# Sliding-window attention with a dense two-layer network behind it: all scores in 64x64 quarters, keys transposed from paired heads, and another order of work in the head

## The chip, the cores and the metric

The kernel runs on one core of one Trainium2 chip. The metric is device time in microseconds (us) of one execution. One matmul engine (TensorE, "PE" in the profile) has a queue of its own, as have VectorE (DVE), ScalarE (ACT), GpSimd (POOL) and SyncE (SP). Each runs its instructions in program order and waits on semaphores for the others. PE reads SBUF and writes the accumulators in PSUM, which has eight banks.

## The reference

q, k and v have 8 batches, 8 heads, 576 positions and 64 channels. Cut to what matters:

```
scores = scale * q @ k.T                       # per batch and head
scores = where(abs(pos_q - pos_k) <= 32, scores, -1e9)
attn   = softmax(scores)                       # over keys
x      = (attn @ v), heads side by side        # 4608 tokens x 512
h      = x @ w_in                              # 512 -> 2048
out    = (h * sigmoid(1.702 * h)) @ w_out      # 2048 -> 512, float32
```

## The kernel before

The 4608 tokens are 36 units of 128 queries, each shifted by 32, so that unit u needs 64 + 64 + 64 keys. A unit has two blocks of 64 queries; each block needs 128 keys. Heads go in pairs: an even head lies on partitions 0 to 63 of `kT` and `qT`, the odd one on 64 to 127.

- `scores(u)` (L200) makes, for four head pairs and two blocks, a tile of keys by queries. In block 0 it does this with two matmuls per head pair, each on 64 rows by 128 columns of the PE array (the profile's form `64*128`, one for each head of the pair). In block 1 it uses four matmuls on 64 by 64 quarters (`64*64`), since there the two halves of the keys lie the other way round. So a unit has 24 matmuls, and the two forms take turns eight times a unit. ScalarE then takes exp (L218), `band(u)` on VectorE multiplies with the mask (L233).
- `values(u)` (L249) multiplies with v; `ve` holds the tokens 128u to 128u+127 and `vo`, which `odd_v` copies out of two `ve` tiles (L136, L137), those shifted by 64. `norm(u)` divides by the sum (L260, L261), and `x_T(u)` transposes x, on PE (L276) or, with no bank named, by a DMA that SyncE issues (L272). Two units make a tile xT[t] of 256 tokens.
- `layer1(t, d)` (L288, L290) is eight matmuls of 256 columns and one gelu; eight such chunks make t. `layer2(u, quarter)` (L299) is four matmuls of 512 columns; behind the fourth quarter VectorE copies the result out of PSUM (L303) and SyncE issues its store.
- `keys_T` and `queries_T` transpose a 512-token group of k and q for one head pair by eight PE transposes of 64 columns each (L145) and copy them into the rings `kT` and `qT`. From group 3 on q goes another way: `queries_cast` (L170) puts the heads of a pair side by side on VectorE, and `queries_X` (L175) transposes the whole group in one DMA. Where a ring wraps, `queries_wrap` (L180) copies its first columns behind its end and for that waits for the group's DMA.

PSUM banks have kinds: "h" (2 banks), "o" (1), "tp" (1), "a" (4). A tile of a kind waits until the last reader of the tile that had its bank is done. The first layer uses "h", the second "o" and "h", scores and values "a".

The order on each engine is written out by hand. `head()` sets up, issues the first loads on GpSimd's DMA queue, does the attention of units 0 to 3 alone, then layer 1 of t = 0 and 1, half of layer 2 of units 0 to 3, then attention of 4 to 6, then the other half. From then on `window(w)`, w = 4 to 19, does the attention of units 2w and 2w+1 around layer 2 of units 2w-4 and 2w-3, and then layer 1 of t = w-1. `feed(w)` prepares the `vo` tiles of the next window.

Of the kernel before, what the change touches and what calls it, by code (L numbers as in the profile page):

```python
# [27 lines left out]
class _Kernel:  # L28
# [29 lines left out]
    def bank(self, kind, shape, dtype, name):  # L58
        bufs = {"h": 2, "o": 1, "a": 4, "tp": 1}[kind]
        return self.ps.tile(shape, dtype, name=name, tag=kind, bufs=bufs)  # L60
# [19 lines left out]
    def setup_mask(self):  # L80

        nc, m = self.nc, self.mask
        lo, hi = slice(0, 64), slice(64, 128)
        nc.vector.memset(m, 1.0)
        for blks, rows, sign in ((slice(0, 2), lo, 1), (slice(0, 2), hi, -1), (slice(2, 4), lo, -1), (slice(2, 4), hi, 1)):
            ap = m[rows, blks, :].rearrange("p b (j s) -> p b j s", j=JT)
            nc.gpsimd.affine_select(out=ap, in_=ap, compare_op=ALU.is_ge, fill=0.0, base=0,
                                    pattern=[[0, 2], [-sign, JT], [-sign * JT, SQ // JT]], channel_multiplier=sign)
        cut = m.rearrange("p b (j s) -> p b j s", j=JT)
        for b, rows, cols in ((0, hi, slice(0, 8)), (0, lo, slice(8, 16)), (2, lo, slice(0, 8)), (2, hi, slice(8, 16))):  # L90
            nc.vector.memset(cut[rows, b, :, cols], 0.0)
# [57 lines left out]
    def keys_T(self, i, hp, kind="tp", eng=None):  # L149
        nc = self.nc  # L150
        tp = self.heads_T("k", i, hp, kind)
        at = (512 * i) % RING

        def put(dst, n):
            self.cast(eng or nc.vector, dst.rearrange("r (p j) -> r p j", j=JT),
                      tp[:, :, :n // JT].rearrange("r j p -> r p j"))

        put(self.kT[:, hp, at:at + 512], 512)
        if at == 0:
            put(self.kT[:, hp, RING:] if i else self.k_first[:, hp, :], 64)  # L160

    def queries_T(self, i, hp, kind="tp", eng=None):
# [4 lines left out]
    def queries_cast(self, i, hp, eng):  # L167
        if ("s", i) not in self.stage:
            self.stage["s", i] = self.work.tile([128, 4, JT, 2, self.D], BF16, name="qc", tag="qc")
        eng.tensor_copy(self.stage["s", i][:, hp],  # L170
                        self.stage["q", i][:, 2 * hp:2 * hp + 2, :].rearrange("p h (j d) -> p j h d", j=JT))

    def queries_X(self, i):
        at = (128 * i) % RP
        self.nc.sync.dma_start_transpose(self.qT[:, :, at:at + 128],  # L175
                                         self.stage["s", i].rearrange("p h j t d -> p (h j t d)"))
# [23 lines left out]
    def scores(self, u):  # L200
# [39 lines left out]
    def values(self, u):  # L240
        nc, D = self.nc, self.D
        p = self.p.pop(u)
        acc = [self.bank("a", [128, 4, D + 1], F32, f"pv{i}") for i in range(2)]
# [71 lines left out]
    def head(self):  # L315

        nc, dve, act = self.nc, self.nc.vector, self.nc.scalar
# [11 lines left out]
        for c in range(4):  # L329
            self.load_w_in(c)  # L330
        for c in range(2):
            self.load_w_out(c)
        for c in "kq":
            self.load_heads(1, c)
        self.load_v(4, 1)
        for m in range(5, 8):
            self.load_v(m)
        for c in range(2, 4):
            self.load_w_out(c)
        for c in "kq":  # L340
            self.load_heads(2, c)
        kinds = ("h", "tp", "h", "o")
        for hp in range(4):
            self.keys_T(0, hp, kinds[(2 * hp) % 4], dve)
            self.queries_T(0, hp, kinds[(2 * hp + 1) % 4], act)
# [8 lines left out]
        self.odd_v(1, dve)  # L354
        self.edge_T("k", "h", dve)
        self.edge_T("q", "h", act)
        self.values(1)
        self.x_T(0, "tp")
        self.norm(1)
        self.band(2)  # L360
        self.scores(3)
        self.odd_v(2, dve)
        self.values(2)
        self.x_T(1, "o")
        self.norm(2)
        self.band(3)
        self.odd_v(3, dve)
        self.values(3)
        self.x_T(2, "tp")
        self.norm(3)  # L370
        self.layer1(0, 0)
        self.x_T(3, "o")
        self.layer1(0, 1)
        self.layer1(1, 0)
        self.layer1(1, 1)
        dve.tensor_copy(self.v_first, self.ve[0][0:64])
        self.queries_wrap(0)
        for c in range(1, 4):
            for t in range(2):
                for d in (2 * c, 2 * c + 1):  # L380
                    self.layer1(t, d)
        kinds = ("h", "h", "o", "tp")
        for c in range(2):
            for u in range(4):
                self.layer2(u, c, kinds[u])
# [5 lines left out]
        self.odd_v(4, dve)  # L391
        self.odd_v(5, dve)
        self.odd_v(6, dve)
# [7 lines left out]
        self.band(6)  # L401
        self.x_T(4, "a")
        self.values(6)
        self.norm(6)
        self.x_T(5, "a")
        for u in range(4):
            self.layer2(u, 2)
        self.x_T(6, "a")
        for u in range(4):
            self.layer2(u, 3)  # L410
        for m in (8, 9, 10):
            self.load_v(m)
        for c in "kq":
            self.load_heads(3, c)
        for d in range(4):
            self.layer1(2, d)
        for hp in range(4):
            self.keys_T(2, hp, ("o", "tp")[hp % 2], dve)
            self.queries_T(2, hp, "a", act)
        for d in range(4, 8):  # L420
            self.layer1(2, d)
        for m in (7, 8, 9):
            self.odd_v(m, dve)
        for m in (11, 12, 13):
            self.load_v(m)

    def window(self, w):
# [3 lines left out]
        l2 = [(lambda u=u, i=i: self.layer2(u, i, ("o", "h")[u % 2]))  # L431
              for u in (2 * w - 4, 2 * w - 3) for i in range(4)]
        l1 = [(lambda d=d: self.layer1(w - 1, d)) for d in range(8)] if w <= self.NW else []
        if w == 4:
            heads = [(3, hp) for hp in range(4)]
        else:
            i = (w + 3) // 2
            heads = [(i, hp) for hp in ((0, 1) if w % 2 else (2, 3))] if 512 * i < self.N else []
# [6 lines left out]
        if w % 2 == 0 and 512 * (w // 2 + 2) < self.N:  # L445
            for c in "kq":
                self.load_heads(w // 2 + 2, c)
        if w == 4:
            self.scores(7)
            run(l2, 1)  # L450
            self.band(7)
        if att:
            self.scores(a)
        if w == 4:
            self.values(7)
            self.norm(7)
            self.x_T(7, "tp")
        for m in (2 * w + 6, 2 * w + 7):
            if 13 < m < self.NU:
                self.load_v(m)  # L460
        if att:
            self.scores(b)
        run(l2, 2)
        if w > 4:
            run(kt)
        run(l2, 2)
        if att:
            self.band(a)
        if w > 4:
            run(kt)  # L470
# [11 lines left out]
        if heads and w % 2:  # L482
            for hp in range(4):
                self.queries_cast(heads[0][0], hp, dve)
        if w == 4:
            for hp in range(4):
                self.queries_cast(3, hp, dve)
            self.queries_X(3)
        run(l2)
        run(l2)  # L490
        run(l1, 4)
        if w == 4:
            run(kt, 4)
        if w % 2 and heads:
            self.queries_X(heads[0][0])
# [66 lines left out]
```

## Time and profile before

| | us |
|---|---|
| median of 3 runs | 381.6 (380.46 to 382.26) |
| the profiled execution | 382.74 |
| its span, first to last instruction | 381.0 |
| PE busy (matmuls) | 347.7 |
| VectorE busy | 146.0 |
| ScalarE busy | 173.3 |
| GpSimd busy | 67.1 |

The span is shorter than the execution's own time by 1.7 us, which lie ahead of its first and behind its last instruction. Busy times are unions of an engine's instructions. The end of a matmul is modelled, so successive matmuls overlap in the rows, and how fast PE really goes is read from start to start. The granted clock is given as a share of 2.4 GHz: 1.00 is that level and 0.50 is 1.2 GHz.

### The profile page before, as it was taken

Reading aid. Unit: us, or ns where it says so; the run is one execution under the profiler, and the core shown is the slowest. Engines: PE = TensorE matmul, PEld = TensorE weight load, DVE = VectorE, ACT = ScalarE, POOL = GpSimd, SP = SyncE. Lnnn points to the kernel's source line nnn. Section 1 sums busy time; section 2 is a strip of 40 time slices with the busy share of each in tenths; the row PEclk is TensorE's granted clock in tenths of the full one; section 3 lists DMA queues with packets and bytes.
Section 4 is the critical chain, followed back from the end, with each engine's and each line's share of the span. In section 5 each row is a group of like instructions: output and inputs, shape, how many; then the busy total and the mean of one; then the engine's idle time right before and its main releaser. Section 6 shows DMA issues by size and latency. Waiting matters only on the chain.

```text
span 381.0 us, 8343 instructions
## 1 busy us (share of the span) xinstructions
PE 347.7 (91%) x3592; PEld 228.6 (60%) x3592; DVE 146.0 (38%) x427; ACT 173.3 (45%) x261; POOL 67.1 (18%) x94
## 2 busy tenths in 40 slices
PE   2849998998768999999999999999999999999995
PEld 1538855574453757575757575748474857666572
DVE  1662037343532525353444434342525250606001
ACT  2523634184242364545454554545463637382250
POOL 8834624100400104020401031110100000000000
PEclk9999995998998999999999999999999999999998
DMA  8999997922990929692969195908090211402011
GB/s 98 177 207 186 198 183 56 136 93 17 104 161 14 116 51 126 102 119 48 127 102 128 40 134 98 146 21 97 24 145 23 61 45 41 58 27 62 28 52 55
DMA packets 94429, 35.27 MB, mean 93 GB/s; under 512 B 67257, under 2 KB 89785, under 8 KB 94393
## 3 DMA queue, kind: packets, MB, share of 16 engines
q0 software_dynamic: 61760, 18.49, 51.4%
q1 hardware_dynamic: 32632, 16.26, 22.5%
q8 instruction: 28, 0.46, 0.5%
q14 instruction: 9, 0.07, 0.0%
HBM read 36.96 MB, written 9.44 MB: 122 GB/s over the span
## 4 chain that ended last, share of the span: by engine, by line
PE 75%; DVE 14%; DMA 6%; issue 2%; ACT 1%; POOL 1%; DVEq 0%; POOLq 0%
PE h_ps L288 31%; PE o_ps L299 29%; PE sc L212 9%; DMA qT<-qc 4%; DVE p L233 3%; DVE x L261 3%; PE pv L249 3%; DVE o_sb L303 3%; PE tp L145 2%; DMA qs<-in_q_dram 2%; DVE qc L170 2%; DVE kT L95 2%; DVE rec L260 1%; PE tp L276 1%; ACT p L218 1%
## 5 line engine op out<-in xcount | busy, mean ns | idle before, releaser
L290 ACT ACTIVATE g<-h_ps 128x512 bf16<-128x512 f32 x144 | 86.0, 597 | 167.8 <-PE h_ps L288 167.8
L299 PE MATMUL o_ps<-w_out_sb,g 128*128 128x512 bf16 x576 | 138.5, 390 | 0.0
L288 PE MATMUL h_ps<-xT,w_in_sb 128*128 128x256 bf16 x1152 | 132.9, 275 | 4.7 <-DVE o_sb L303 4.7
L288 PEld LDWEIGHTS <-w_in_sb 128*128 128x128 bf16 x1152 | 113.6, 99 | 23.9 <-issue 5.8
L299 PEld LDWEIGHTS <-g 128*128 128x128 bf16 x576 | 53.5, 100 | 61.7 <-issue 5.9
L95 DVE COPY kT<-tp 128x512 bf16<-128x512 bf16 (+2 forms) x45 | 25.6, 594 | 120.7 <-PE tp L145 120.7
L129 POOL DMA_DIRECT2D ve<-in_v_dram x40 | 33.8, 853 | 198.8 <-DVE rec L260 125.1
L303 DVE COPY o_sb<-o_ps 128x512 f32<-128x512 f32 x36 | 24.8, 689 | 75.7 <-PE o_ps L299 74.6
L212 PE MATMUL sc<-qT,kT 64*64 64x64 bf16 (+1 forms) x864 | 44.9, 215 | 2.3 <-DVE qT L180 2.3
L218 ACT ACTIVATE p<-sc 128x512 bf16<-128x512 f32 x70 | 36.7, 600 | 11.2 <-PE sc L212 11.1
L212 PEld LDWEIGHTS <-kT 64*64 64x64 bf16 (+1 forms) x864 | 30.9, 102 | 18.1 <-issue 6.0
L261 DVE TENSOR_TENSOR x<-pv,rec 128x256 bf16<-128x256 f32 x72 | 30.5, 424 | 2.5
L233 DVE TENSOR_TENSOR p<-p,mask 128x512 bf16<-128x512 bf16 x70 | 26.5, 418 | 6.0 <-ACT p L218 5.5
L249 PEld LDWEIGHTS <-p 128*64 128x64 bf16 x576 | 14.3, 118 | 18.6 <-DVE p L233 9.1
L145 PE MATMUL tp<-ident,ks 128*64 128x128 bf16 x288 | 15.8, 234 | 10.1 <-DMA ks<-in_k_dram 7.1
L249 PE MATMUL pv<-ve,p 128*64 128x65 bf16 x288 | 19.2, 208 | 5.7 <-DVE p L233 3.8
L145 PEld LDWEIGHTS <-ks 128*64 128x64 bf16 x288 | 10.4, 115 | 20.9 <-issue 9.7
L249 PE MATMUL pv<-vo,p 128*64 128x65 bf16 x288 | 18.5, 207 | 3.2 <-DVE vo L137 2.7
L290 ACT ACT_TABLE_LOAD x16 | 20.5, 1283 | 0.3
L218 ACT ACT_TABLE_LOAD x15 | 19.2, 1283 | 0.3
L95 ACT COPY qT<-tp 128x512 bf16<-128x512 bf16 (+1 forms) x13 | 7.2, 570 | 16.6 <-PE tp L145 16.4
L260 DVE RECIPROCAL rec<-pv 128x4 f32<-128x4 f32 x72 | 12.5, 173 | 2.2 <-PE pv L249 1.9
(36 smaller groups left out, 93.0 us busy)
## 6 DMA issues: line engine op xcount, KB each, us to landing
out_dram<-o_sb SPq DMA_DIRECT2D x70, 128.0 KB
ve<-in_v_dram POOLq DMA_DIRECT2D x32, 128.0 KB, 5.3
w_in_sb<-in_moe_w_in_dram POOLq DMA_DIRECT2D x4, 512.0 KB, 9.8
w_out_sb<-in_moe_w_out_dram POOLq DMA_DIRECT2D x4, 512.0 KB, 12.1
ks<-in_k_dram POOLq DMA_DIRECT2D x4, 256.0 KB, 6.1
qs<-in_q_dram POOLq DMA_DIRECT2D x4, 256.0 KB, 7.4
ks<-in_k_dram POOLq DMA_DIRECT2D x2, 448.0 KB, 13.8
qs<-in_q_dram POOLq DMA_DIRECT2D x2, 448.0 KB, 14.8
```

The lines of the kernel that those rows point to most:

```text
L95: (eng.copy if eng is self.nc.scalar else eng.tensor_copy)(out, in_)
L129: self.nc.gpsimd.dma_start(self.ve[m % NV][off:off + n, :, :self.D], self.v[b, :, s:s + n, :].rearrange("h s d -> s h d"))
L145: self.nc.tensor.transpose(tp[64 * t:64 * t + 64, j, :], self.stage[c, i][:, 2 * hp + t, j * self.D:(j + 1) * self.D], self.ident)
L212: nc.tensor.matmul(sc[eo][lo:lo + m, 2 * hp + blk, :], self.kT[r, hp, at:at + m], self.qT[r, JT * hp:JT * hp + JT, q0:q0 + 16], start=(n = ...
L218: nc.scalar.activation(p[:, eo], sc[eo], AF.Exp, scale=self.scale)
L233: self.nc.vector.tensor_mul(pv, pv, msk.to_broadcast([128, 4, 2, SQ]))
L249: nc.tensor.matmul(acc[half][blk * 64:blk * 64 + 64, hh, :], p[:, h % 2, h // 2 * 2 + blk, :], vt[:, h, :D + 1], start=(hh == 0), stop=(hh ...
L261: nc.vector.tensor_mul(x[:, hs, :], acc[half][:, :, :D], rec[:, hs, :].to_broadcast([128, 4, D]))
L288: nc.tensor.matmul(hps[:, i, :], self.w_in_sb[:, kr, ff * 128:(ff + 1) * 128], self.xT[t][:, kr, :], start=(i == 0 and kr == 0), stop=(i = ...
L290: nc.scalar.activation(self.g[t][:, 2 * d:2 * d + 2, :], hps, AF.Gelu_apprx_sigmoid)
L299: nc.tensor.matmul(o_ps, self.g[t][:, ff, s * 128:(s + 1) * 128], self.w_out_sb[:, ff, :], start=(ff == 0), stop=(ff == self.NFF - 1))
L303: nc.vector.tensor_copy(o_sb, o_ps)
```

## The change

It has four parts.

1. `scores` uses four 64x64 quarters in both blocks: 32 matmuls a unit and one form.
2. Keys of groups 3 and later are first put side by side by head pair on VectorE (`pair_heads`, the former `queries_cast`), and then transposed by four full 128x128 transposes.
3. The head is put in another order: the four `odd_v` of units 0 to 3 and the mask's memsets go to GpSimd, between the loads; layer 1 begins after units 0 and 1, with units 2 and 3 between its first chunks; attention of units 4 to 6 stands between chunks of layer 2 ("output-layer atoms"); the attention of window 4 (units 7 to 9) likewise.
4. In the windows, pairing q and its DMA go from between norm and the last layer-2 chunks into `feed`, behind `odd_v`, with the pairing of k; the loads of k and q stand a group earlier.

```diff
 # scores(u)
-                parts = ((0, 64, k0 + 64), (64, 64, k0)) if blk else ((0, 128, k0),)
-                for lo, m, at in parts:
+                for half in range(2):
+                    lo, at = 64 * half, k0 + 64 * (half ^ blk)
                     for eo in range(2):
                         r = slice(eo * 64, eo * 64 + 64)
-                        nc.tensor.matmul(sc[eo][lo:lo + m, 2 * hp + blk, :], self.kT[r, hp, at:at + m],
+                        nc.tensor.matmul(sc[eo][lo:lo + 64, 2 * hp + blk, :], self.kT[r, hp, at:at + 64],
 # keys_T(i, hp)
+        if ("k", i, "c") in self.stage:
+            tp = self.bank(kind, [128, JT, 128], BF16, "tp")
+            for j in range(JT):
+                self.nc.tensor.transpose(tp[:, j, :], self.stage["k", i, "c"][:, hp, j], self.ident)
+        else:
+            tp = self.heads_T("k", i, hp, kind)
 # pair_heads(c, i, hp, eng), was queries_cast
+        eng.tensor_copy(self.stage[c, i, "c"][:, hp],
+                        self.stage[c, i][:, 2 * hp:2 * hp + 2, :].rearrange("p h (j d) -> p j h d", j=JT))
 # head(): loads
+        self.load_w_in(0)
+        self.load_w_in(1)
+        self.odd_v(0, pool)
+        self.odd_v(1, pool)
+        self.load_w_in(2)
+        self.odd_v(2, pool)
+        self.odd_v(3, pool)
+        self.load_w_in(3)
+        self.cut_mask()
...
 # head(): the start of the work
         self.scores(0)
         self.scores(1)
+        self.edge_T("k", "h", dve)
+        self.edge_T("q", "h", act)
         self.band(0)
-        self.odd_v(0, dve)
         self.band(1)
         self.scores(2)
-        self.values(0)
+        self.values(0, "hh")
         self.norm(0)
...
+        self.scores(3)
+        self.values(1, "ot")
         self.norm(1)
+        self.x_T(0, "h", act)
+        self.x_T(1, "h", act)
         self.band(2)
+        self.layer1(0, 0)
         self.values(2)
         self.norm(2)
         self.band(3)
+        self.layer1(0, 1)
         self.values(3)
         self.norm(3)
+        self.layer1(0, 2)
+        self.x_T(2, "t")
+        self.layer1(0, 3)
         self.x_T(3, "o")
...
 # head(): run(n) issues the next n chunks of layer 2 of units 0 to 3
+        run(4)
         for hp in range(4):
             self.keys_T(1, hp, "a", dve)
             self.queries_T(1, hp, "a", act)
+            run(1)
         self.scores(4)
         self.scores(5)
...
         self.band(4)
+        run(3)
         self.band(5)
+        run(2)
         self.values(4)
         self.norm(4)
         self.scores(6)
+        self.band(6)
+        run(1)
         self.values(5)
         self.norm(5)
+        run(1)
         self.x_T(4, "a")
+        run(1)
+        self.x_T(5, "a")
...
+        self.layer1(2, 0)
         self.values(6)
         self.norm(6)
+        for d in range(1, 3):
+            self.layer1(2, d)
         self.x_T(6, "a")
+        self.layer1(2, 3)
         for hp in range(4):
+            self.keys_T(2, hp, "t", dve)
+            self.queries_T(2, hp, "o", act)
+            self.layer1(2, 4 + hp)
 # window(4): scores(7), scores(8), then two layer-2 chunks, and so on, with a chunk or two between
+            self.values(b)
+            self.norm(b)
+            self.x_T(b)
+            loads()
+            run(l2, 2)
+            run(l1, 2)
+            for c in "qk":
+                for hp in range(4):
+                    self.pair_heads(c, 3, hp, dve)
+                if c == "q":
+                    self.queries_X(3)
+            run(l1, 3)
+            for _ in range(3):
+                run(kt)
+                run(l1)
+            run(kt)
+            self.feed(w)
 # feed(w), behind odd_v and ahead of queries_wrap
+        heads = self.heads(w + 1)
+        for i, hp in heads:
+            self.pair_heads("k", i, hp, dve)
+        if w % 2 and self.heads(w):
+            i = self.heads(w)[0][0]
+            for hp in range(4):
+                self.pair_heads("q", i, hp, dve)
+            self.queries_X(i)
```

## Rows read from the trace of the kernel before

**Rows 1.** Page, part 1: busy us (share of the span) and instructions.

```profile
PE 347.7 (91%) x3592; PEld 228.6 (60%) x3592; DVE 146.0 (38%) x427; ACT 173.3 (45%) x261; POOL 67.1 (18%) x94
```

**Rows 2.** Stages: length, busy us of PE, PEld, DVE, ACT, POOL; clock; DMA.

```profile
13.20:29.26 16.06, 10.98 (x182) 7.65 (x181) 10.28 (x33) 6.58 (x11) 7.72 (x11) 1.00 1.39 199
29.26:46.09 16.83, 16.83 (x135) 14.22 (x134) 2.17 (x8) 8.96 (x15) 8.60 (x11) 1.00 1.55 192
46.09:83.09 37.00, 35.02 (x388) 22.03 (x388) 18.07 (x45) 14.96 (x24) 9.44 (x13) 0.86 1.04 122
83.09:111.62 28.53, 22.71 (x253) 14.16 (x253) 12.95 (x37) 10.60 (x16) 5.34 (x7) 0.94 0.82 88
111.62:134.55 22.93, 20.03 (x194) 12.37 (x194) 8.14 (x25) 9.51 (x14) 1.77 (x2) 0.93 0.61 75
134.55:302.51 167.96, 164.73 (x1731) 107.49 (x1730) 69.71 (x201) 84.67 (x126) 22.30 (x28) 1.00 0.76 90
302.51:355.72 53.21, 52.37 (x530) 35.05 (x530) 18.43 (x55) 29.57 (x42) 0.00 (x0) 1.00 0.22 46
355.72:381.00 25.28, 20.87 (x128) 12.32 (x126) 2.77 (x4) 5.38 (x9) 0.00 (x0) 0.96 0.13 42
```

**Rows 3.** Chain that ended last: start us, us, what.

```profile
100.66 14.36 DMA qT<-qc
...
172.00 2.31 PE sc L212 x48
...
183.29 7.06 PE h_ps L288 x64
...
369.68 6.92 PE o_ps L299 x32
```

**Rows 4.** Timeline of PE in a window: start us, us, operation, shapes.

```profile
176.08 0.41 PE L145 MATMUL tp<-ident,ks 128*64 128x128 bf16 x8
176.43 1.90 PE L299 MATMUL o_ps<-w_out_sb,g 128*128 128x512 bf16 x8
...
181.23 0.19 PE L249 MATMUL pv<-vo,p 128*64 128x65 bf16 x1
...
181.26 0.19 PE L249 MATMUL pv<-vo,p 128*64 128x65 bf16 x1
181.39 1.90 PE L299 MATMUL o_ps<-w_out_sb,g 128*128 128x512 bf16 x8
```

**Rows 5.** Groups by line and form, quarters of the scores: busy us, mean ns.

```profile
L212 PE MATMUL sc<-qT,kT 64*64 64x64 bf16 x576 | 33.2, 220 | 2.3 <-DVE qT L180 2.3
L212 PEld LDWEIGHTS <-kT 64*64 64x64 bf16 x576 | 16.9, 106 | 8.6 <-issue 2.3
```

**Rows 6.** Timeline of PE: four full transposes, and the matmuls behind them.

```profile
69.86 0.39 PE L276 MATMUL tp<-ident,x 128*128 128x128 bf16 x4
70.08 3.62 PE L299 MATMUL o_ps<-w_out_sb,g 128*128 128x512 bf16 x16
```

**Rows 7.** Timeline of VectorE in the same window as rows 4.

```profile
178.36 0.69 DVE L303 COPY o_sb<-o_ps 128x512 f32<-128x512 f32 x1 [1.14 <-PE o_ps L299]
...
180.24 0.75 DVE L233 TENSOR_TENSOR p<-p,mask 128x512 bf16<-128x512 bf16 x2
```

**Rows 8.** Waits: who waited for whom, us in total, times, longest us.

```profile
PE h_ps L288 <- DVE o_sb L303: 4.7, 6, 2.1
```

**Rows 9.** Timeline of VectorE in the head: the second unit's last norm.

```profile
22.22 0.42 DVE L261 TENSOR_TENSOR x<-pv,rec 128x256 bf16<-128x256 f32 x1
```

**Rows 10.** Groups by line: copies on VectorE, and mask work on GpSimd.

```profile
L136 DVE COPY vo<-ve 64x528 bf16<-64x528 bf16 x36 | 11.4, 318 | 0.8
...
L170 DVE COPY qc<-qs 128x512 bf16<-128x512 bf16 x24 | 6.1, 317 | 0.0
...
L87 POOL TENSOR_SCALAR_AFFINE_SELECT mask<-mask 64x128 bf16<-64x128 bf16 x4 | 1.5, 364 | 0.2
```

**Rows 11.** DMA issues: count, KB each, median us from issue to landing.

```profile
w_in_sb<-in_moe_w_in_dram POOLq DMA_DIRECT2D x4, 512.0 KB, 9.8
```

More of the change, by code (lines that the diff above doesn't have):

```diff
@@ L80, in setup_mask, with cut_mask @@
     def setup_mask(self):
-        nc, m = self.nc, self.mask
+        pool, m = self.nc.gpsimd, self.mask
         lo, hi = slice(0, 64), slice(64, 128)
-        nc.vector.memset(m, 1.0)
+        pool.memset(m, 1.0)
         for blks, rows, sign in ((slice(0, 2), lo, 1), (slice(0, 2), hi, -1), (slice(2, 4), lo, -1), (slice(2, 4), hi, 1)):
             ap = m[rows, blks, :].rearrange("p b (j s) -> p b j s", j=JT)
-            nc.gpsimd.affine_select(out=ap, in_=ap, compare_op=ALU.is_ge, fill=0.0, base=0,
-                                    pattern=[[0, 2], [-sign, JT], [-sign * JT, SQ // JT]], channel_multiplier=sign)
-        cut = m.rearrange("p b (j s) -> p b j s", j=JT)
+            pool.affine_select(out=ap, in_=ap, compare_op=ALU.is_ge, fill=0.0, base=0,
+                               pattern=[[0, 2], [-sign, JT], [-sign * JT, SQ // JT]], channel_multiplier=sign)
+    def cut_mask(self):
+        cut = self.mask.rearrange("p b (j s) -> p b j s", j=JT)
+        lo, hi = slice(0, 64), slice(64, 128)
         for b, rows, cols in ((0, hi, slice(0, 8)), (0, lo, slice(8, 16)), (2, lo, slice(0, 8)), (2, hi, slice(8, 16))):
-            nc.vector.memset(cut[rows, b, :, cols], 0.0)
+            self.nc.gpsimd.memset(cut[rows, b, :, cols], 0.0)
     def cast(self, eng, out, in_):
@@ L147, in heads_T, with keys_T, queries_T @@
         return tp
-    def keys_T(self, i, hp, kind="tp", eng=None):
-        nc = self.nc
-        tp = self.heads_T("k", i, hp, kind)
+    def keys_T(self, i, hp, kind="t", eng=None):
+        if ("k", i, "c") in self.stage:
[4 more added lines that the diff above has]
+            tp = self.heads_T("k", i, hp, kind)
         at = (512 * i) % RING
         def put(dst, n):
-            self.cast(eng or nc.vector, dst.rearrange("r (p j) -> r p j", j=JT),
+            self.cast(eng or self.nc.vector, dst.rearrange("r (p j) -> r p j", j=JT),
                       tp[:, :, :n // JT].rearrange("r j p -> r p j"))
         put(self.kT[:, hp, at:at + 512], 512)
-        if at == 0:
-            put(self.kT[:, hp, RING:] if i else self.k_first[:, hp, :], 64)
-    def queries_T(self, i, hp, kind="tp", eng=None):
+        if at == 0 and i:
+            put(self.kT[:, hp, RING:], 64)
+    def queries_T(self, i, hp, kind="t", eng=None):
         at = (128 * i) % RP
@@ L165, in queries_T, with pair_heads @@
         self.cast(eng or nc.vector, self.qT[:, JT * hp:JT * hp + JT, at:at + 128], tp)
[L167 to L171, printed above, removed]
+    def pair_heads(self, c, i, hp, eng):
+        if (c, i, "c") not in self.stage:
+            self.stage[c, i, "c"] = self.work.tile([128, 4, JT, 2, self.D], BF16, name=c + "c", tag=c + "c")
+        eng.tensor_copy(self.stage[c, i, "c"][:, hp],
+                        self.stage[c, i][:, 2 * hp:2 * hp + 2, :].rearrange("p h (j d) -> p j h d", j=JT))
     def queries_X(self, i):
@@ L175, in queries_X @@
         self.nc.sync.dma_start_transpose(self.qT[:, :, at:at + 128],
-                                         self.stage["s", i].rearrange("p h j t d -> p (h j t d)"))
+                                         self.stage["q", i, "c"].rearrange("p h j t d -> p (h j t d)"))
     def queries_wrap(self, i):
@@ L238, in band, with values @@
                     self.nc.vector.tensor_mul(pv, pv, msk.to_broadcast([128, 4, SQ // JT, JT]))
-    def values(self, u):
+    def values(self, u, kinds="aa"):
         nc, D = self.nc, self.D
         p = self.p.pop(u)
-        acc = [self.bank("a", [128, 4, D + 1], F32, f"pv{i}") for i in range(2)]
+        acc = [self.bank(kinds[i], [128, 4, D + 1], F32, f"pv{i}") for i in range(2)]
         for half in range(2):
@@ L315, in head @@
     def head(self):
-        nc, dve, act = self.nc, self.nc.vector, self.nc.scalar
+        nc, dve, act, pool = self.nc, self.nc.vector, self.nc.scalar, self.nc.gpsimd
         self.setup()
@@ L328, in head @@
         self.load_v(4, 0)
-        for c in range(4):
-            self.load_w_in(c)
+        self.load_w_in(0)
[7 more added lines that the diff above has]
+        self.cut_mask()
         for c in range(2):
@@ L334, in head @@
             self.load_heads(1, c)
+        self.load_w_out(2)
         self.load_v(4, 1)
@@ L337, in head @@
             self.load_v(m)
-        for c in range(2, 4):
-            self.load_w_out(c)
+        self.load_w_out(3)
         for c in "kq":
             self.load_heads(2, c)
[L342 to L345, printed above, removed]
+        kinds = "htho"
+        for half in (0, 2):
+            for hp in (half, half + 1):
+                self.keys_T(0, hp, kinds[hp], dve)
+            for hp in (half, half + 1):
+                self.queries_T(0, hp, kinds[hp ^ 2], act)
@@ L374, in head @@
-        self.layer1(1, 0)
-        self.layer1(1, 1)
+        for d in range(4):
+            self.layer1(1, d)
         dve.tensor_copy(self.v_first, self.ve[0][0:64])
+        dve.tensor_copy(self.k_first, self.kT[:, :, 0:64])
         self.queries_wrap(0)
[L378 to L385, printed above, removed]
+        for t in range(2):
+            for d in range(4, 8):
+                self.layer1(t, d)
@@ L386, in head, with run @@
+        l2 = [(lambda c=c, u=u: self.layer2(u, c, "hhot"[u])) for c in range(4) for u in range(4)]
+        def run(n):
+            for _ in range(n):
+                l2.pop(0)()
+        run(4)
         for hp in range(4):
@@ L388, in head @@
             self.queries_T(1, hp, "a", act)
+            run(1)
         self.scores(4)
         self.scores(5)
-        self.odd_v(4, dve)
-        self.odd_v(5, dve)
-        self.odd_v(6, dve)
+        for m in range(4, 7):
+            self.odd_v(m, dve)
         self.band(4)
+        run(3)
         self.band(5)
+        run(2)
         self.values(4)
@@ L398, in head @@
         self.scores(6)
+        self.band(6)
+        run(1)
         self.values(5)
         self.norm(5)
-        self.band(6)
+        run(1)
         self.x_T(4, "a")
+        run(1)
+        self.x_T(5, "a")
+        self.load_v(8)
+        self.load_v(9)
+        self.load_v(10)
+        for c in "kq":
+            self.load_heads(3, c)
+        self.layer1(2, 0)
         self.values(6)
         self.norm(6)
-        self.x_T(5, "a")
-        for u in range(4):
-            self.layer2(u, 2)
+        for d in range(1, 3):
+            self.layer1(2, d)
         self.x_T(6, "a")
[L409 to L416, printed above, removed]
+        self.layer1(2, 3)
         for hp in range(4):
[L418 to L421, printed above, removed]
+            self.keys_T(2, hp, "t", dve)
+            self.queries_T(2, hp, "o", act)
+            self.layer1(2, 4 + hp)
         for m in (7, 8, 9):
@@ L425, in head, with heads @@
             self.load_v(m)
+        for c in "kq":
+            self.load_heads(4, c)
+    def heads(self, w):
+        if w == 4:
+            return [(3, hp) for hp in range(4)]
+        i = (w + 3) // 2
+        return [(i, hp) for hp in ((0, 1) if w % 2 else (2, 3))] if 512 * i < self.N else []
     def window(self, w):
@@ L430, in window @@
         att = w < self.NW
-        l2 = [(lambda u=u, i=i: self.layer2(u, i, ("o", "h")[u % 2]))
+        l2 = [(lambda u=u, i=i: self.layer2(u, i, "oh"[u % 2]))
               for u in (2 * w - 4, 2 * w - 3) for i in range(4)]
         l1 = [(lambda d=d: self.layer1(w - 1, d)) for d in range(8)] if w <= self.NW else []
[L434 to L438, printed above, removed]
+        heads = self.heads(w)
         kt = [lambda i=i, hp=hp: self.keys_T(i, hp) for i, hp in heads]
@@ L443, in run, with loads @@
                 lst.pop(0)()
-        if w % 2 == 0 and 512 * (w // 2 + 2) < self.N:
-            for c in "kq":
-                self.load_heads(w // 2 + 2, c)
+        def loads():
+            for m in (2 * w + 6, 2 * w + 7):
+                if m < self.NU:
+                    self.load_v(m)
+            if w % 2 == 0 and 512 * (w // 2 + 3) < self.N:
+                for c in "kq":
+                    self.load_heads(w // 2 + 3, c)
         if w == 4:
             self.scores(7)
-            run(l2, 1)
+            self.scores(a)
+            run(l2, 2)
             self.band(7)
+            self.scores(b)
+            run(l2)
+            self.band(a)
+            run(l2)
+            self.values(7)
+            self.norm(7)
+            self.band(b)
+            run(l2)
+            self.x_T(7, "t")
+            self.values(a)
+            self.norm(a)
+            self.x_T(a)
+            run(l2)
+            self.values(b)
+            self.norm(b)
+            self.x_T(b)
+            loads()
+            run(l2, 2)
+            run(l1, 2)
[10 more added lines that the diff above has]
+            self.feed(w)
+            return
+        loads()
         if att:
             self.scores(a)
[L454 to L461, printed above, removed]
+            if w > 5:
+                self.scores(b)
+        run(l2, 2)
+        run(kt)
+        run(l2)
+        if w == 5:
             self.scores(b)
[L463 to L466, printed above, removed]
+        run(l2)
         if att:
             self.band(a)
-        if w > 4:
-            run(kt)
+        run(kt)
         run(l2)
@@ L481, in window @@
             self.x_T(b)
[L482 to L490, printed above, removed]
+        run(l2, 2)
         run(l1, 4)
[L492 to L495, printed above, removed]
         self.feed(w)
```

14 lines of the change are left out of this document (1 added, 13 removed).

## The prediction

> **What bounds the kernel now.** I read the page's first part before anything else: PE is busy 91% of the span, the next engine 45% [rows 1]. That says PE, but not whether the time goes into arithmetic. So I then took the span stage by stage [rows 2]. From 134.55 on PE is never idle for long (164.73 of 167.96 us) at full clock: nine windows of 18.66 us. Before that lies the loose part: 5.1 us of 16.06 idle while the first attention runs alone, and 2.0, 5.8 and 2.9 us idle in the next three attention stages, where the mean clock also fell to 0.86, 0.94 and 0.93. The chain of waits says the same: in the windows it runs through PE nearly all the way, and its one long foreign piece is the 14.36 us of the query transpose by DMA [rows 3]. So two things can give time: cheaper PE work in all windows, and the holes before 134.55.
>
> **Prices.** Chunk of layer 1: 7.06/8 = 0.88. Chunk of layer 2: 6.92/8 = 0.865. The scores of two units: 48 matmuls in 2.31 us, in 16 groups (head pair and block), so 0.144 a group for 64 columns [rows 3]. That is dear, and the timeline shows why. Values matmuls, also in pairs side by side, follow each other at 0.03 us while the form stays (181.23 to 181.26); the step to the next form takes 0.13 (181.26 to 181.39) [rows 4]. A change of form thus costs about 0.10, and scores change form at every group.
>
> **Part 1, scores.** With one form a group should cost 0.144 - 0.10 = 0.045, between the 0.03 of the values pairs (lower end) and 0.144 (upper end of the case in which weights still load during matmuls, no gain). No row shows two quarter groups in a row, so this is an estimate; I take 0.045, since it comes from the scores' own rows. Two units then cost 15 x 0.045 + 0.144 = 0.82 in place of 2.31, 1.49 less a window. At 0.03 it is 1.72, at 0.144 nothing. There are eight more matmuls a unit, but within a group they are already issued side by side.
>
> The Trainium skill, page "TensorE: Matmul & The Clock Gate", section "Part 3: Packing small matmuls", speaks against it: a weight load is said to overlap running matmuls only where their row group differs, and both blocks use both row groups. Our values pairs, which use all rows each time, still start 0.03 us apart [rows 4], so the rule doesn't hold for them; by it a group would be load and matmul in series, which the third rival prices from rows.
>
> That price: 0.220 for a quarter's matmul plus 0.106 for its weight load, 0.33 a group [rows 5].
>
> **Part 2, keys.** A head pair's key transposes take 0.35 now (176.08 to 176.43) plus the 0.10 of a form change back [rows 4]; four full ones take 0.22 (69.86 to 70.08) in the form of the layers around them [rows 6]. That is 0.2 less, twice in each of nine windows. The second of the two gains nothing. Behind the fourth layer-2 chunk VectorE runs copy, two masks, key copy, two masks without a hole from 178.36 to 180.99 [rows 7], 2.63 us, and values of the second unit wait for its end; PE has less to do meanwhile and comes earlier to the same wait. So 0.2 a window. The pairing of keys adds 24 copies of 0.25 to 0.32 us [rows 10] on VectorE, beside the 7.06 us of layer 1, at nothing; without that cover it would cost up to 7.6.
>
> **Part 4, pairing of q moved.** Layer 1 waits six times for the copy that frees its bank, 4.7 us in all [rows 8], where four pairing copies stand ahead of that copy. I credit 2 us to the windows after 134.55; the rest lies in windows 4 and 5, which I sum anew. In `feed` the pairing stands behind `odd_v` (1.2 us later) and SyncE issues its DMA later, two windows ahead of its use.
>
> **Windows 6 to 17.** Nine windows: 167.96 - 9 x (1.49 + 0.2) - 2 = 150.7. Three without keys: 53.21 - 3 x 1.49 = 48.7. The end, 25.28, stays [rows 2].
>
> **Part 3, the head.** Up to 13.20 it is loads, unchanged.
> - First attention: unit 1's norm ends at 22.64 [rows 9]. Of what stands ahead of it on VectorE, two `odd_v` (1.2 us) and a copy of xT (0.4) leave; transposing x and copying it adds about 1. Layer 1 thus begins near 21.6 rather than 29.26. Lower end 20.5.
> - Its upper end is 26, and that is GpSimd. No row has a copy on GpSimd: VectorE's takes 0.3 [rows 10], and GpSimd's select, 0.364 for 128 elements, scaled to 528 gives 1.5. I take 0.9 between ends so far apart with nothing nearer. Eight copies put the third and fourth load of w_in up to 7 us later in that queue, with w_out and everything else behind. w_in lands 9.8 us after issue [rows 11]; chunks that need the last one start after 33, so this is covered. If the first masks wait for the memsets that now stand behind the fourth load (other blocks of the same tile), they run at 20 to 21 and not 16: 4 to 5 us.
> - Layer 1 of t = 0, 1: the 16.83 us it takes now (part of it at the lower clock), plus values of two units at 0.51 with their form change, two x transposes and 0.9 of waits: 19.2. Ends at 40.8.
> - 46.09 to 83.09 now takes 37.0. The work: 16 layer-2 chunks 13.8, 8 layer-1 chunks 7.1, 16 transposes of keys and queries at 0.35 (5.6), scores 3 x 0.56, values 3 x 0.51, x transposes 0.7; 30.4. VectorE has four output copies among masks and norms just ahead of layer 1, and I add 3.4 for waits: 33.8. Ends at 74.6.
> - Window 4, now 28.53: layer 2 6.9, layer 1 7.1, scores 1.7, values 1.5, keys 0.9, x 0.2, waits 1: 19.3. Ends at 93.9.
> - Window 5, now 22.93: a later window's 18.66 - 1.69, and 0.1 for scores taken apart: 17.1. Ends at 111.0, 23.6 before 134.55. The transpose of the third query group is issued after two layer-1 chunks; should it again take 14.36, VectorE stands some 4 us at the wrap copy behind it, with key copies and masks queued, and window 5 is longer by that.
>
> Sum: 111.0 + 150.7 + 48.7 + 25.3 = 335.7 span. The profiled execution lies 1.7 above its span, 337.4; that execution was 1.1 above the median of the runs shown, 336.3. The head's sums assume full clock once layer 1 runs; the old trace fell to half after a hole in each attention stage [rows 2], so I allow 0.7 and say 337.
>
> A second rule is weighed with the 0.9: "GPSIMD Engine Reference", section "Key points", of the Trainium skill says that GpSimd shares SBUF interfaces with VectorE and contends with its fast copies. No row here has such a copy; it would lengthen both, within the 26 above.
>
> **The rivals.**
> 1. Quarters don't stream: with weights loaded during the matmuls but the groups no faster than 0.144, 18 windows of two units lose their 1.49, 27 us: 364. For it: no two quarter groups ever stand in a row. Against: the values pairs.
> 2. The head stays loose: masks wait for the memsets (5), the wrap copy for its DMA (4), VectorE's queue ahead of layer 1 (3), and a stretch of half clock (3): 352. For it: VectorE's order in rows 7 already decides a window. Against: PE has 1 to 3 us of chunks between each pair of steps.
> 3. The other side: weights wait for the matmul in the same rows, 0.33 a group. Each of 288 groups costs 0.186 more than now, 53.6 us, against about 19 gained elsewhere: 416. It turns slower above 0.144 + 19/288 = 0.21 a group. Against it stand the values pairs again.
>
> **Chances.** Forecast 0.74 (its own range 330 to 345), first rival 0.08, second 0.15, third 0.03. The range that holds eight in ten reaches from 329 (0.03 a group gives 4 less, the early start 1, no waits 3) to 355, with the second rival inside. A measurement of this kernel can't tell less than 0.5% from no change. Only the third rival is slower: faster 0.96, same 0.01, slower 0.03.
>
> **What would show it.** In the changed profile, score groups of two units within 0.7 to 0.9 us and all in the 64x64 form; first layer-1 matmul at 21 to 22; first scores of window 6 near 111 and windows of 17 us behind it; the clock at 1.00 from 40 on; values still waiting for the second mask. I am wrong if the groups stay at 0.14, or if window 6 starts later than 120.

## The result and the profile after

The changed kernel takes 341.2 us, median of four runs (340.39 to 342.43), against 381.8 before: a ratio of 0.895, 95% interval 0.891 to 0.898. Forecast were 337 and a range of 329 to 355. Of all the executions below one, the fourth of the kernel with doubled scores (370.6 us), fell into a slower state of the chip, and its figures leave it out. The page's first part, the granted clock and the group of the layer-2 matmuls of the changed kernel:

```profile
PE 304.7 (90%) x3748; PEld 207.4 (61%) x3784; DVE 146.6 (43%) x433; ACT 174.1 (51%) x263; POOL 73.0 (22%) x107
...
PEclk9999999999978999999999999999999999999999
...
L308 PE MATMUL o_ps<-w_out_sb,g 128*128 128x512 bf16 x540 | 129.0, 381 | 6.8 <-issue 6.3
```

PE is busy 43 us less than in [rows 1] and still 90% of its span; the span shrank with its work. Not all of the 43 is saved work: the records of 36 layer-2 matmuls (540 of 576) are missing from this trace, and gaps of up to 0.16 us, 4.8 us in all, stand where they should be. So PE is really busy some 38 us less. The stages, as in [rows 2] (length, busy us of PE, PEld, DVE, ACT, POOL, clock, DMA), cut at the start of layer 1, of layer 2, of windows 4, 5, 6 and 15, and behind window 17:

```profile
12.70:21.34 8.64, 6.27 (x178) 4.55 (x177) 5.06 (x15) 6.57 (x14) 8.11 (x17) 1.00 1.54 187
21.34:39.50 18.16, 17.64 (x168) 14.48 (x168) 4.19 (x15) 10.21 (x16) 10.18 (x14) 1.00 1.33 196
39.50:70.93 31.43, 29.44 (x410) 17.91 (x412) 16.88 (x41) 15.09 (x24) 13.48 (x18) 1.00 1.54 179
70.93:90.61 19.68, 18.62 (x258) 12.09 (x260) 12.66 (x40) 10.72 (x17) 5.34 (x7) 1.00 0.87 115
90.61:115.92 25.31, 17.61 (x199) 11.54 (x200) 11.13 (x35) 9.18 (x14) 4.62 (x6) 0.87 1.05 83
115.92:265.82 149.90, 143.60 (x1783) 99.13 (x1800) 72.60 (x217) 84.68 (x126) 19.63 (x24) 1.00 0.99 101
265.82:314.00 48.18, 46.38 (x571) 31.88 (x577) 18.43 (x55) 29.57 (x42) 0.00 (x0) 1.00 0.21 51
314.00:339.50 25.50, 20.93 (x128) 12.42 (x127) 2.77 (x4) 5.38 (x9) 0.00 (x0) 1.00 0.13 42
```

One line stands out: window 5 (90.61 to 115.92) takes 25.31 us, with PE idle for 7.7 of them and the only clock below 1.00; windows 7 to 14 take 16.5 to 16.6. Before, window 5 began at 111.62, now 21 us earlier, but window 6 is only 18.6 us earlier. The timeline of PE there, and that of VectorE:

```profile
94.25 0.22 PE L221 MATMUL sc<-qT,kT 64*64 64x64 bf16 x4
101.56 0.59 PE L221 MATMUL sc<-qT,kT 64*64 64x64 bf16 x28 [7.09 <-DVE qT L189]
```

```profile
101.31 0.20 DVE L189 COPY qT<-qT 128x128 bf16<-128x128 bf16 x1 [8.11 <-DMA qT<-qc]
```

Scores of unit 11 begin, stop after one group, and wait 7.09 us for the wrap copy, which waits for the third query group's DMA. In the chain of waits, where [rows 3] had 14.36 us of it and 2.31 us of scores, the changed kernel has:

```profile
84.98 16.30 DMA qT<-qc
...
183.43 0.67 PE sc L221 x64
```

So the transfer is no faster than before, and what was hidden ahead of it is gone. Behind the wait PE goes at half clock for 3 us:

```profile
101.56:104.56 3.00, 2.78 (x36) 1.62 (x37) 1.09 (x2) 2.35 (x3) 0.00 (x0) 0.50 0.00 0
```

The scores of two units are 64 matmuls in 0.67 us, in 16 groups.

### The profile page after: what moved, and what is told of

The parts are those of the page before. It is cut to its first block, busy times and chain, and to the rows that moved or that the text cites. A ratio compares the mean times of both kernels' runs of the same rounds, so it can differ in the third digit from the quotient of the medians.

```text
span 339.5 us, 8719 instructions
## 1 busy us (share of the span) xinstructions
PE 304.7 (90%) x3748; PEld 207.4 (61%) x3784; DVE 146.6 (43%) x433; ACT 174.1 (51%) x263; POOL 73.0 (22%) x107
## 4 chain that ended last, share of the span: by engine, by line
PE 74%; DVE 12%; DMA 7%; issue 3%; POOL 2%; ACT 1%; POOLq 0%; ACTq 0%
PE h_ps L297 37%; PE o_ps L308 30%; DMA qT<-qc 5%; DVE p L242 4%; DVE o_sb L312 3%; PE sc L221 3%; PE pv L258 3%; DMA edge<-in_k_dram 2%; DVE kT L99 2%; PE tp L149 1%; DVE x L270 1%; PE tp L158 1%; POOL ve L133 1%; DVE p L247 1%; ACT p L227 1%
## 5 line engine op out<-in xcount | busy, mean ns | idle before, releaser
L308 PE MATMUL o_ps<-w_out_sb,g 128*128 128x512 bf16 x540 | 129.0, 381 | 6.8 <-issue 6.3
L297 PEld LDWEIGHTS <-w_in_sb 128*128 128x128 bf16 x1152 | 112.4, 98 | 21.5 <-issue 2.5
L308 PEld LDWEIGHTS <-g 128*128 128x128 bf16 x576 | 52.5, 98 | 57.5 <-issue 2.9
L133 POOL DMA_DIRECT2D ve<-in_v_dram x40 | 33.8, 851 | 161.3 <-PE pv L258 98.1
L227 ACT ACTIVATE p<-sc 128x512 bf16<-128x512 f32 x70 | 36.4, 602 | 12.8 <-PE sc L221 12.7
L221 PE MATMUL sc<-qT,kT 64*64 64x64 bf16 x1152 | 15.3, 200 | 7.6 <-DVE qT L189 7.1
L258 PEld LDWEIGHTS <-p 128*64 128x64 bf16 x576 | 13.7, 115 | 13.8 <-DVE p L242 8.5
L221 PEld LDWEIGHTS <-kT 64*64 64x64 bf16 x1152 | 12.7, 113 | 12.4 <-issue 12.0
L227 ACT ACT_TABLE_LOAD x15 | 19.2, 1283 | 0.3
L258 PE MATMUL pv<-vo,p 128*64 128x65 bf16 x288 | 18.6, 203 | 0.7 <-DVE p L247 0.6
L127 POOL DMA_DIRECT2D qs<-in_q_dram x17 | 12.3, 731 | 3.4 <-DMA w_out_sb<-in_moe_w_out_dram 1.8
L127 POOL DMA_DIRECT2D ks<-in_k_dram x17 | 12.2, 723 | 2.0 <-DMA qs<-in_q_dram 1.2
```

The lines of the kernel that those rows point to most:

```text
L127: self.nc.gpsimd.dma_start(self.stage[key][off // JT:(off + m) // JT, lo:hi, :], src[b, lo:hi, s:s + m, :].rearrange("h (p j) d -> p h (j ...
L133: self.nc.gpsimd.dma_start(self.ve[m % NV][off:off + n, :, :self.D], self.v[b, :, s:s + n, :].rearrange("h s d -> s h d"))
L221: nc.tensor.matmul(sc[eo][lo:lo + 64, 2 * hp + blk, :], self.kT[r, hp, at:at + 64], self.qT[r, JT * hp:JT * hp + JT, q0:q0 + 16], start=(n ...
L227: nc.scalar.activation(p[:, eo], sc[eo], AF.Exp, scale=self.scale)
L258: nc.tensor.matmul(acc[half][blk * 64:blk * 64 + 64, hh, :], p[:, h % 2, h // 2 * 2 + blk, :], vt[:, h, :D + 1], start=(hh == 0), stop=(hh ...
L297: nc.tensor.matmul(hps[:, i, :], self.w_in_sb[:, kr, ff * 128:(ff + 1) * 128], self.xT[t][:, kr, :], start=(i == 0 and kr == 0), stop=(i = ...
```

## The experiments

My theory: the scores were dear because of the change of form and nothing else; the head's new order gives a good part of the rest; window 5 loses some 8 us to one DMA that shares its engines with loads. All kernels below were timed beside the kernel before. "Before" and "changed" are the two kernels above. Windows are from the first scores of one to those of the next.

**Quarter scores alone, and everything but them.** The first edit is the diff's first hunk in the kernel before, the second that hunk taken back in the changed kernel.

> The kernel before with one edit: scores in 64x64 quarters in both blocks. Theory: alternating forms cost the scores about 0.11 us a group; without that two units take 0.67 us in place of 2.31, 1.64 less in each of 18 pairs, less about 2 where the first attention waits for exp anyway: 27 us, so 355 us. Rival A, the head's order brought nearly all of the gain and faster scores only come earlier to the masks: above 375. Rival B, both parts need each other (faster scores let VectorE set the end of each window): 365 to 370.

> The changed kernel with the old scores (64x128 in block 0, quarters in block 1). Theory: the same 1.64 us a pair comes back, 27 us in all, 368 us, windows near 18.1 us. Rival A: under 348, since the rest of the gain is the head's. Rival B: 350 to 358.

Measured: 357.3 us (ratio to before 0.940, 0.936 to 0.944) and 365.9. The scores alone take 23.3 us off the 380.6 of the kernel before, timed beside them, and taken out of the changed kernel they cost 24.7. The chain of the kernel with the old scores has, in each window:

```profile
249.25 2.31 PE sc L221 x48
```

Its windows take 18.11 us against 16.47, so 1.64 a pair, as expected. Both rivals are out: the two parts add up. I expected 27 in all. Of what is missing in the trace of the run with the old scores, 1.4 lies in window 6, which took 18.11 there and 17.90 in the changed kernel's trace because of a halt that I come to at the end; some 1.0 lies in windows 4 and 5 and the rest ahead of them.

**Is it the change of form, or the 64x128 form itself?** The old two forms, with the loops swapped:

```diff
-        for hp in range(4):
-            for blk in range(2):
+        for blk in range(2):
+            for hp in range(4):
```

> The changed kernel with the old two forms, but all four groups of block 0 first and then all four of block 1, so that the form changes twice a unit and not eight times. Theory (a change of form costs about 0.11 us, the forms themselves nothing): two units take 12 groups of 0.031 and 4 of 0.13 to 0.15, 0.93 us, 0.26 above the all-quarter scores, 18 times: 346 us. Rival (the 64x128 form is dear in itself, 0.13 a group wherever it stands): two units take 8 x 0.13 + 8 x 0.031 and a change or two, 1.4 us: 354 us.

Measured: 343.8 us, windows of 16.75. In its chain:

```profile
250.95 0.94 PE sc L221 x48
```

0.94, as the price of a change of form says (0.93), not 1.4. The matmuls are those that took 2.31; only their order differs. That settles it: 12 changes of form fewer for two units are worth 1.37 us, 0.11 each.

**The price of a quarter group by itself.** Every score matmul twice (`for again in range(2):` around the loops).

> The changed kernel with every score matmul issued twice, the second pass over the first: the price of a quarter group by itself. Theory (0.031 a group, as the new trace's start times suggest): 16 more groups a pair, 0.5 us, 18 times, 9 us: 350 us. The price that I had forecast, 0.045: 13 us, 354. If the matmuls were cheap only because the engine waits for something else anyway: under 344.

Measured: 362.1 us (361.4 to 366.4), a miss. The group itself came out cheap, 128 matmuls in

```profile
250.28 1.22 PE sc L222 x128
```

that is 0.034 for each of the 16 added groups, and quiet windows take 17.03 us (250.21 to 267.24), 0.56 more than the changed kernel's. But windows 8 and 10 took 19.6 and 20.6, and the first layer-1 chunk began at 25.5. In its timeline PE stands still in the middle of such work, waiting for nothing that the profile shows:

```profile
171.48 1.70 PE L298 MATMUL h_ps<-xT,w_in_sb 128*128 128x256 bf16 x14 [2.44 <-issue]
```

```profile
205.72 0.26 PE L259 MATMUL pv<-ve,p 128*64 128x65 bf16 x1 [1.96 <-issue]
```

The added matmuls explain 18 x 0.55 = 10 us of the 20.3 by which this trace's execution is above the changed kernel's; most of the rest goes with such halts. The longest are two of 1.56 and 3.86 us ahead of layer 1, with a stretch of half clock behind them, and the two above. More on them at the end.

**The wait of window 5.** Three ways to take it away: issue the transpose 20 us earlier, do it on PE, or take the competing load away.

```diff
 # a_early: in head(); window(4) then pairs k alone and has no queries_X(3)
         self.x_T(6, "a")
+        for hp in range(4):
+            self.pair_heads("q", 3, hp, dve)
+        self.queries_X(3)
         self.layer1(2, 3)
 # a_pe: in window(4), which then has no pairing of q and no queries_X(3)
-            run(l1, 3)
-            for _ in range(3):
+            run(l1, 2)
+            for hp in range(4):
                 run(kt)
+                self.queries_T(3, hp, "o", nc.scalar)
                 run(l1)
-            run(kt)
 # a_lateload: load_heads(5) from window 4 to window 6, behind load_v
```

> The changed kernel with the pairing and the DMA transpose of the third query group issued in the head, ahead of the fourth layer-1 chunk of tile 2, some 20 us earlier. Theory (window 5's 25.3 us against my 17.1 are the 7.1 us that PE waits for this transpose behind the wrap copy, and the stretch at half clock that follows): window 5 near 17 us, 333 us. Rival A (the same transfer now meets the loads of group 4 and is late all the same, or its four copies hold up the keys): above 339. Rival B (behind the transpose the next wait in window 5 is as late): window 5 above 20 us, 337.

> The changed kernel with the third query group transposed on PE in window 4 (eight half transposes a head pair, copied by ScalarE), without its DMA. Theory: no wait at the wrap copy, at a price of 4 x 0.45 us on PE: window 4 near 21.5, window 5 near 17, 335 us. Rival (window 5 was held by VectorE's key copies and not by the DMA): window 5 stays above 20 us, above 339.

> The changed kernel with the load of group 5 of k and q put two windows later in GpSimd's queue, behind the v tiles of window 6; nothing else moves. Theory C (the transpose takes 16.3 us because the loads share its DMA engines): it lands 7 to 9 us after issue, the wait at the wrap copy goes from 7.1 to under 1, 334 us. Rival D (it takes 16 us by itself, its descriptors alone take SyncE 9.6): wait 5 us or more, 340.

Measured: 338.3, 332.9 (ratio to before 0.874, 0.868 to 0.881) and 337.7, where the theory had 333, 335 and 334. On PE it went as the theory has it, and cost less. Windows 4 and 5 of that kernel:

```profile
71.53:92.36 20.83, 19.91 (x290) 13.27 (x292) 13.02 (x40) 12.63 (x20) 5.33 (x7) 1.00 1.00 112
92.36:109.02 16.66, 16.33 (x198) 10.98 (x200) 9.94 (x32) 9.52 (x14) 4.67 (x6) 1.00 1.09 88
```

Window 4 is 1.15 us longer (20.83 against 19.68), window 5 is 16.66 in place of 25.31, and no half clock is left there. The other two took the wait out of window 5 as well (17.0 in both, with scores of 11 at once) but lost time elsewhere. With the early transpose PE halts 3.4 us amid the scores of window 4, again with nothing named, while the DMA runs; a stretch of half clock follows, and the window takes 25.28:

```profile
74.81 0.54 PE L221 MATMUL sc<-qT,kT 64*64 64x64 bf16 x24 [3.38 <-issue]
```

With the late load, SyncE issued the third group's transpose in 5.87 us (9.61 in the changed kernel), and it was no longer late: it landed 8.0 us after issue, not 16.3. But the moved load met the next one, of group 4: its piece in the chain, and the scores of window 7 behind it:

```profile
106.13 24.11 DMA qT<-qc
```

```profile
130.28 0.46 PE L221 MATMUL sc<-qT,kT 64*64 64x64 bf16 x28 [4.12 <-DMA qT<-qc]
```

That is the contention theory shown from both sides: take the load away and the transfer is in time; put it beside another transfer and that one takes 24 us. The fourteen traces (the two kernels and twelve runs) bear it out: they have 82 of these transposes, and the 44 with a load of k or q under way in their first 5 us took 12.7 to 24.1 us from issue to landing, the 38 without one 5.6 to 8.3. The total was then no better than 337.7, so rival D's number came nearer by chance.

**Keys and the pairing of q.** Keys by eight half transposes again (`heads_T` for all groups, no pairing of k); and the pairing of q put back ahead of the last two layer-2 chunks.

> The changed kernel with keys of all groups transposed as before, eight half transposes a head pair, and without their pairing on VectorE. My prediction: 0.2 us a window in nine windows and 0.9 in window 4, 2.7 in all, 344 us. Rival A (both key transposes of a window count): windows 0.45 longer, 5 in all, 346. Rival B (it gives nothing, VectorE sets the window): 341.

> The changed kernel with the pairing of q back between norm and the last layer-2 chunks of the odd windows (its DMA behind the first four layer-1 chunks). My prediction credited 2 us in the windows behind window 6, where the old trace had waits of 4.7 us in six: four windows longer by 0.5 to 0.8, 343.5 us. Rival (the output copy comes early enough without it): 341, windows of 16.5 all along.

Measured: 346.0 and 346.4. With half transposes windows with keys take 16.70 against 16.47, 0.23 more: only one of a window's two head pairs counts, as I had it. In window 4, where I had put 0.9, it is 0.2 (19.86 against 19.68). The rest of its 4.8 us is not the keys': in its trace layer 1 began 1.8 us later behind a halt of 1.76, and window 10 was 1.3 us longer with another, so I don't credit more than about 2.5 to the keys. That the total is rival A's is chance. The pairing was under-sized. Its waits line:

```profile
PE h_ps L297 <- DVE o_sb L312: 3.9, 5, 1.2
```

The odd windows 7, 9, 11 and 13 took 17.4, 17.9, 17.0 and 17.0, together 3.3 us above the changed kernel's; I had credited 2 from [rows 8]. Window 5 took 26.7, but 25.3 and 26.0 in two executions of the changed kernel, so I don't count it.

**The new order by itself.** All parts but the head and window 4, in the kernel before. One more thing of the change is not in this run: its loads of k and q stand where they stood before, and not a group earlier.

> The kernel before with everything of the change but the new order of the head and of window 4: quarter scores, keys from paired heads, pairing of q in feed. From 357.3 us with quarter scores alone: keys 0.23 us in eight windows and 0.9 in window 4, pairing 0.5 to 0.8 in four windows: 352. Theory (the new order gives a good part of the rest by itself): it lies 9 to 12 above the changed kernel's 341.2. Rival (the order gives little, the parts made up for it): below 346.

Measured: 351.3, 10.1 above the changed kernel; the rival is out. The 10.1 are the new order's with the earlier loads. Its windows 4 and 5:

```profile
80.70:108.90 28.20, 20.03 (x258) 12.68 (x260) 14.68 (x43) 10.49 (x16) 5.33 (x7) 0.94 0.87 92
108.90:127.40 18.50, 16.13 (x199) 11.10 (x200) 8.63 (x27) 9.41 (x14) 1.76 (x2) 1.00 0.76 91
```

The new order begins window 5 at 90.61 in place of 108.90, 18.3 us ahead, and then needs 25.31 us for it against 18.50: 6.8 are given back to the DMA that now has too little time. The earlier loads have a side effect: the transposes of groups 4 to 6 took 6.2 to 7.6 us in this run and 13.7 to 15.3 in the changed kernel, where loads of k and q run beside them. Nobody waits for those, since they are issued two windows ahead.

**A better version, and the same once more.** On top of the PE transposes: `load_edge` ahead of `setup_mask`, and `x_T(4, "a", act)`, `x_T(5, "a", act)`.

> The third query group on PE as in the run at 332.9 us, and two further edits in the head: the two edge loads issued ahead of the mask's setup (the chain has the first masks wait for the edge keys' DMA from 9.16 to 15.22), and x of units 4 and 5 copied out of PSUM by ScalarE in place of VectorE (PE waits 1.8 us at 60.5 behind VectorE's output copies). Theory: 0.7 to 1 us from the first, 0.4 to 0.7 from the second: 331.5. Rival (exp and w_in's landing set the start of layer 1, and the norm and not the copy the other): 333.

> The changed kernel once more, unchanged, on the chip of these runs: 341 within 1.5 us. It says how far a difference of 2 us between runs may be read.

Measured: 332.1 (ratio to before 0.872, 0.869 to 0.876) and 341.2. It beats both kernels by a clear margin. By the totals the two further edits can't be told from the run at 332.9, but the stages tell them apart. ScalarE's copy shortened the wait ahead of layer 1 (1.57 to 0.67 us), and the stage from layer 2 to window 4, which took 31.42 to 31.43 in seven runs without this edit, took 0.9 less:

```profile
40.01:70.54 30.53, 29.43 (x411) 17.90 (x413) 16.16 (x39) 16.26 (x26) 13.54 (x18) 1.00 1.54 182
```

The edge keys were no earlier, PE still waited 1.1 us for them. The repeat differs from the first by 0.04 us in the median, while single stages moved by more: layer 1 began at 22.4 behind a halt of 1.25, and window 6 had none.

What the parts are worth, then: scores 23 to 25, keys and pairing 6.0 (357.3 to 351.3), the new order with the earlier loads 10.1, after window 5 had taken 6.8 of it back.

## Why the prediction was right

Its terms and what the trace has for them:

| term | predicted us | measured us |
|---|---|---|
| layer 1 begins | 21.6 | 21.34 |
| layer 1 of t = 0, 1 | 19.2 | 18.16 |
| to window 4 | 33.8 | 31.43 |
| window 4 | 19.3 | 19.68 |
| window 5 | 17.1 | 25.31 |
| windows 6 to 14 | 150.7 | 149.90 |
| windows 15 to 17 | 48.7 | 48.18 |
| the end | 25.3 | 25.50 |

- Bound: right. PE's work set the windows (windows 6 to 17 gave 23.1 us), and the holes ahead of them were the other half (18.6).
- Scores: the mechanism was right, the size a little off. A group costs 0.031, my lower end, and not 0.045; two units take 0.67 against my 0.82. Reading the price off the scores' own rows as the remainder of a subtraction was worse than taking it from the neighbour that already ran without changes of form. The rule of the Trainium skill ("TensorE: Matmul & The Clock Gate", section "Part 3: Packing small matmuls") that a weight load overlaps only matmuls of another row group is not borne out here: successive quarter groups use both row groups and still go at 0.031, where load and matmul in series would have made 0.33. The third rival and the first fell with it, and the run that doubled the matmuls has 0.034 for a group by itself.
- Windows 6 to 14 came out close to the sum (149.90 against 150.7) because the cheaper scores (9 x 0.15) and the pairing, which gave 3.3 and not 2, made up for window 6: it took 17.90 with a halt of 1.82 in it, which the repeat did not have (16.47).
- Keys: right for the windows, 0.23 each. VectorE still sets the end of values, from

```profile
187.91 0.69 DVE L312 COPY o_sb<-o_ps 128x512 f32<-128x512 f32 x1 [0.90 <-PE o_ps L308]
...
189.92 0.75 DVE L242 TENSOR_TENSOR p<-p,mask 128x512 bf16<-128x512 bf16 x2
```

  to the end of the second mask at 190.67, 2.76 us, in place of the 2.63 in [rows 7]; the second unit's values go on at 190.73.
- Head: each stage right within about 1 us up to window 5, except that waits before window 4 were put 2.4 too high. GpSimd's copies took 0.65 and not 0.9, and the first masks, at 15.90, did not wait for the memsets, which GpSimd did at 20.61 (groups by line, then the timelines of the two engines):

```profile
L140 POOL COPY vo<-ve 64x528 bf16<-64x528 bf16 x4 | 2.6, 659 | 0.2
L141 POOL COPY vo<-ve 64x528 bf16<-64x528 bf16 x4 | 2.6, 642 | 0.2
```

```profile
15.90 2.12 DVE L242 TENSOR_TENSOR p<-p,mask 128x512 bf16<-128x512 bf16 x4
```

```profile
20.61 0.51 POOL L95 MEMSET mask<- 64x32 bf16 x4
```

  The Trainium skill's rule of shared SBUF interfaces ("GPSIMD Engine Reference", section "Key points") can't be judged from this: the first four masks, beside these copies, took 2.12 us from 15.90 on, 0.53 each against a mean of 0.43, which would agree, but nothing here tells it from other causes.
- The step that failed is "Window 5 ... 17.1". I had named the wait, priced it at some 4 and left it out of the sum. PE's wait was 7.1 and VectorE's at the wrap copy 8.1, since the transfer took 16.30, and PE's idle time was followed by 3 us at 0.5 of the clock, in which the work behind took longer: 25.31 in place of 17.1. The working had a visible flaw: the window ahead of it was shortened by 9 us in the same sum, and that time had covered the transfer. The old trace had the transfer at 14.36, and by the sum's own terms it started near 88 in the new order (93.9 less six layer-1 chunks and the keys), which meant an end near 102.
- The wrong sizes largely cancel: window 5 8.2 too low, all other terms together 4.4 too high. That 337 came within 1.3% of 341.2 is in that part luck.

## What to carry to other kernels

- Look at what the matmuls next to each other have in common: where two tile forms alternate, start-to-start times of a group against those of a run in one form price the change at once, and grouping by form (here two swapped loops) already gives 1.37 of the 1.64 us.
- When a schedule is tightened, list each transfer with its old time from issue to landing and check it against the new distance to its first reader; what was covered by the slack that goes is late next.
- Moving a load out of one transfer's way can put it into another's, as it did here; taking the transfer off the DMA engines cost 1.15 us on PE and gained 8.3 net.

## What the runs showed of the hardware that was not expected

PE halts with no wait behind them: 1.56, 3.86, 2.44 and 1.96 us in the run with doubled scores, 3.38 in window 4 with the early transpose, 1.82 in window 6 of the changed kernel and not in its repeat, which has one of 1.25 ahead of layer 1. They are not bound to one instruction. In five runs one comes behind the 223rd matmul on record, whatever stands next there: a values matmul in four of them, a score in the run with doubled scores. The repeat and that run:

```profile
19.75 0.26 PE L258 MATMUL pv<-vo,p 128*64 128x65 bf16 x1 [1.25 <-issue]
```

```profile
16.70 0.51 PE L222 MATMUL sc<-qT,kT 64*64 64x64 bf16 x41 [1.56 <-issue]
```

They go with PE's own program, which comes by DMA as well. The instruction queue moves it in packets of 16 KB, 28 in the kernel before and 38 with doubled scores, one for some 257 matmuls and weight loads in the first and 259 in the second. The fourteen traces have 13 such halts above 0.7 us, and 11 of them end 1.3 to 1.5 us after one of these packets has landed. So in these PE very likely waited for its program. For the other two, 1.82 and 3.38, no packet is on record in the 4 us ahead of their end, and their cause stays open. No run took this apart.

The transpose DMA of one query group took 5.6 to 8.3 us with no load of k or q under way, and 12.7 to 24.11 beside one. SyncE's issue of it stretches along, from 5.87 to 9.61 us in the pair above.
